# Routing operations of an attention + mixture-of-experts kernel that read one operand from PSUM instead of two from SBUF

## The chip, the cores and the metric

The kernel runs on one core of one Trainium2 chip. The metric is the device time of one execution in microseconds (us); a time is the median of several runs.

## The reference

The first half is chunked attention over 4 batches, 8 heads, 768 positions and head size 64, with chunks of 32 queries, a context of 16 positions to the left and 8 to the right, and 8 memory keys. Its output, as 3072 tokens of 512 values, goes through a mixture of 8 experts. Tokens are assigned greedily: all 3072 x 8 logits are sorted, and each token goes to the first expert on the list that still has room, with 384 tokens per expert:

```python
logits = x @ w_gate
order = np.argsort(-logits.flatten())
for idx in order:
    tok, e = (int(idx) // E, int(idx) % E)
    if assigned[tok] >= 0 or counts[e] >= cap:
        continue
    assigned[tok] = e
    counts[e] += 1
...
for e in range(E):
    mask = assigned == e
    h = np.maximum(x[mask] @ w1[e], 0.0)
    out[mask] = h @ w2[e]
```

## The kernel before

The kernel works in two stages. In the **attention** stage (`attention`, some 105 us) 24 tiles of 128 tokens pass through scores, softmax, the product with the values and the logits; each tile's rows are written to a DRAM tensor `xs`.

In the **expert** stage the 8 experts follow each other. For each expert k, `phase` finds in four rounds of counting (r = 0 to 3) which expert fills up next and at which logit, and then which tokens it gets. All its arithmetic is on VectorE (DVE), with small TensorE (PE) matmuls for sums over partitions. The end of a phase is the part that matters here. It goes, in program order: the masks `oe`, `gq`, `gt`; a running sum over the 24 tiles (the scan, L537); two PE matmuls for the offsets of the partitions (L546, L547); the slot numbers (L552 to L561); and three 0/1 tables: `one` (L564), `lo` (L567) and `hi` (L571). `tokens` multiplies `lo` and `hi` on PE (L586), turns the product into token numbers `ids`, gathers the tokens' rows with GpSimd (POOL) indirect DMAs (L603) and transposes them, for k = 0 on PE (L623), later by DMA (L615).

Meanwhile `weights` converts expert weights: ScalarE (ACT) takes sums of absolute values (L695), PE transposes them (L700), DVE makes a power of two, PE spreads it over the partitions (L707), ACT scales and rounds the weights to fp16 (L728, L730), and POOL subtracts to get the low half (L742; two SBUF inputs of 128x1024 in fp32). `gemm` then runs 96 matmuls into `ps_hid` (L795) and 72 into `ps_y` (L810) per expert; ACT and DVE split the hidden values (L759, L762), DVE scales the output (L770) and POOL scatters it (L818).

The order on every engine is fixed when the program is built. `Lines` holds a generator per activity; each yields an engine, a cost and the time at which it can start, and `Lines.run` takes the line that can start first, ties being broken by the ready time less a lead (`soon`, or the line's own). Costs are estimates of the author; they set the order and nothing else. Each engine executes its queue strictly in this order, so a PE matmul of the routing stands in the same queue as the matmuls of the previous expert's `gemm`. For expert 0, where PE would idle by the plan, `fill` adds matmuls that nobody reads (L426, 128 columns each), written to `g.D[:, 384:512]`.

Two PSUM tiles of one bank each hold the routing's small results. `g.D` is written by PE (counts, sums, offsets, pair products, the weight scales, the fill) and read by DVE and ACT. `g.R` (class `Scratch`) is a work area that only DVE writes and reads. The framework orders accesses to a tile by semaphores.

In five of the operations both tensor inputs lie in SBUF: the scan L537 (`g.one48`, `gq`), `s1` L557 (`slot`, `gt`), `one` L564 (`sm`, `g.io`), `lo` L567 (`one`, `g.idc`) and `hi` L571 (`su`, `g.io`). Most other operations of the routing have one input in `g.R` or `g.D`.

Of the kernel before, what the change touches and what calls it, by code (L numbers as in the profile page):

```python
# [11 lines left out]
F32 = mybir.dt.float32  # L12
F16 = mybir.dt.float16
BF16 = mybir.dt.bfloat16
I32 = mybir.dt.int32
AF = mybir.ActivationFunctionType
ALU = mybir.AluOpType
AX = mybir.AxisListType

P = 128  # L20
# [4 lines left out]
NT = N // P  # L25
DM = H * D
E, FF = 8, 1024
CAP = N // E
# [26 lines left out]
def attention(g):  # L55
# [158 lines left out]
    def hist(i):  # L214
        g.first[1].open(g)
        finish(st["early"])

    def keys(i):
        finish(first_keys(g, i - 3, i + 1))
# [12 lines left out]
    for f, i in ((scores, n), (ptrans, n - 1), (softmax, n), (xtrans, n - 3),  # L232
                 (av, n - 2), (ptrans, n), (logits, n - 4), (rows, n - 3), (av, n - 1), (av, n), (logits2, n - 4),
                 (early, 0), (xtrans, n - 2), (logits, n - 3), (xtrans, n - 1), (logits, n - 2), (early, 1),
                 (xtrans, n), (logits, n - 1), (logits, n), (early, 2), (logits2, n), (hist, 0), (keys, n)):
        f(i)
# [8 lines left out]
class Scratch:  # L245
# [5 lines left out]
                e8=(496, 504), ce=(504, 512),  # L251
                sc=(0, 48), sl=(48, 72), slot=(72, 96), gr=(96, 120))

# [125 lines left out]
class Lines:  # L379
# [42 lines left out]
    def fill(self, t):  # L422
        g = self.g
        n = int((t - self.clk[PE] - 0.25) / 0.17)
        for _ in range(n):
            g.nc.tensor.matmul(g.D[:, 384:512], g.ones, g.fill, start=True, stop=True)  # L426


def phase(g, k, out):
# [6 lines left out]
    def t(shape, dt, tag, bufs=1):  # L436
        return rb.tile(shape, dt, tag=tag, name=tag, bufs=bufs)
# [110 lines left out]

    e = yield DVE, 1.8, max(d, p + LATE)
    sl0 = t([P, NT], F32, "sl0")  # L550
    for a, o in enumerate((sl0, R.sl)):
        v.scalar_tensor_tensor(o, sc[:, a], off[:, a:a + 1], gq[:, a], op0=ALU.add, op1=ALU.mult)  # L552
    slot, row = t([P, NT], F32, "slot"), R.gr
    v.tensor_tensor(slot, R.sl, sl0, op=ALU.add)
    s1 = t([P, NT], F32, "s1")
    v.tensor_scalar(row, slot, -7.5, 0.0625, op0=ALU.add, op1=ALU.mult)
    v.scalar_tensor_tensor(s1, slot, float(CAP), gt, op0=ALU.is_lt, op1=ALU.mult)  # L557
    v.tensor_scalar(row, row, HALF, -HALF, op0=ALU.add, op1=ALU.add)
# [3 lines left out]
    e = yield DVE, 0.85, e  # L562
    one = t([P, 6, 16, 4], BF16, "one")
    v.tensor_tensor(one, sm.rearrange("p (j c) -> p j c", c=4).unsqueeze(2).to_broadcast([P, 6, 16, 4]),  # L564
                    g.io[:, 0:16, 0:4].unsqueeze(1).to_broadcast([P, 6, 16, 4]), op=ALU.is_equal)
    lo = t([P, 6, 2, 16, 4], BF16, "lo")
    v.tensor_tensor(lo, one.unsqueeze(2).to_broadcast([P, 6, 2, 16, 4]),  # L567
                    g.idc.unsqueeze(3).to_broadcast([P, 6, 2, 16, 4]), op=ALU.mult)
    e = yield DVE, 0.4, e
    hi = t([P, NT, NT], BF16, "hi")  # L570
    v.tensor_tensor(hi, su.unsqueeze(1).to_broadcast([P, NT, NT]), g.io[:, 1:NT + 1], op=ALU.is_equal)  # L571
    g.lines.add(tokens(g, k, out, lo, hi, e), 0.4)
# [6 lines left out]
def tokens(g, k, out, lo, hi, e):  # L579
# [3 lines left out]
    p = yield PE, 0.45, e + SEM, soon  # L583
    pair = g.D[:, 132:228]
    for j in range(0, NT, 4):
# [25 lines left out]
    for a in range(NG):  # L611
# [7 lines left out]
        bank = "CBA"[a]  # L619
        p = yield PE, 0.55, lambda: max(g.lines.free(bank), at[a]), soon  # L620
        px = g.lines.take(bank, [P, 2 * KC, P], "ps_xg", F16)
# [64 lines left out]
def weights(g, k, st, n):  # L686
# [5 lines left out]
    for j in range(4):  # L692
        t = yield ACT, 1.25, lambda: fl[j][1] if len(fl) > j else INF, due
        jk = g.wbuf.tile([P, 1024], F16, tag="jk16", name="jk16", bufs=1)
        nc.scalar.activation(jk, fl[j][0], AF.Abs, accum_out=am[:, j:j + 1])  # L695
    soon = 0.0 if k else 5.0
    t = yield DVE, 0.15, t + SEM, soon
    v.tensor_reduce(am[:, 4:5], am[:, 0:4], axis=AX.X, op=ALU.max if n == "1" else ALU.add)
    t = yield PE, 0.12, t + SEM
    nc.tensor.transpose(g.D[0:1, 256:256 + P], am[:, 4:5], g.ident)  # L700
# [4 lines left out]
    pr = pow2(g, rb, m, [1, 1], top, name, bufs=1)  # L705
    t = yield PE, 0.1, t + SEM
    nc.tensor.matmul(g.D[:, 128:130], g.one_row, pr.rearrange("p a b -> p (a b)"), start=True, stop=True)  # L707
    t = yield ACT, 0.17, t + LATE
    s = rb.tile([P, 2], F32, tag=name + "s", name=name + "s", bufs=3)
    nc.scalar.activation(s, g.D[:, 128:130], AF.Copy)  # L710
    st["s" + n] = s
# [138 lines left out]
def constants(g, consts):  # L850
# [15 lines left out]
    def cast(n, dt, rows=P):  # L866
        t = g.fixed.tile([rows, c[n].shape[1]], dt, name="c_" + n)
        nc.gpsimd.tensor_copy(t, c[n][:rows])
        return t
# [6 lines left out]
    nc.gpsimd.memset(g.rz, 0.0)  # L876
    g.idc = cast("idc", BF16).rearrange("p (j x c) -> p j x c", x=2, c=4)
    g.put = cast("put", BF16)
# [7 lines left out]
    nc.vector.memset(R.z0, 0.0)  # L886
    g.one48 = g.fixed.tile([P, 2 * NT], F32, name="one48")
    nc.vector.memset(g.one48, 1.0)
    nc.vector.memset(g.one48[:, NT:NT + 1], 0.0)
    nc.vector.tensor_copy(R.e8, g.e8)  # L890
    g.io = g.fixed.tile([P, NT + 1, NT], BF16, name="io")
    g.fill = g.io[:, 0:6].rearrange("p a b -> p (a b)")[:, 0:128]
    for a, b in ((0, 13), (13, NT + 1)):
        yield
        nc.gpsimd.tensor_copy(g.io[:, a:b], c["io"][:, a:b].unsqueeze(2).to_broadcast([P, b - a, NT]))

# [153 lines left out]
```

## Time and profile before

| | |
|---|---|
| median of 3 runs | 483.92 us (482.54 to 483.98) |
| the profiled execution | 480.79 us, of it 479.0 us span from the first to the last instruction |
| PE busy, whole span | 410.0 us (86%) |
| ACT, DVE, POOL busy | 311.4, 302.6 and 255.8 us |
| attention, span start to about 105 us | DMA bound (share 0.92 in its first 103 us) |
| routing of expert 0 alone | about 105 to 155 us, mean PE clock 0.60 |
| experts | about 155 to 470 us, then the last rows leave |

The times below are us from the start of the span. The clock is the granted TensorE clock, where 1.00 is 2.4 GHz and 0.50 is 1.2 GHz. A row of a timeline gives the start, the duration, the engine, the line, the operation, output <- inputs, shapes, the count of merged instructions and, in brackets, the idle time of the engine before it and what ended it.

### The profile page before, as it was taken

The page shows a single profiled execution, that of the slowest core. Times are in us where ns is not written, and L with a number is a line of the kernel's source. Part 1 is how long each engine was busy: PE and PEld are TensorE (multiplying, and loading weights), DVE is VectorE, ACT ScalarE, POOL GpSimd, SP SyncE. Part 2 cuts the span into 40 slices and gives each one's busy share as a digit, 9 for nine tenths or more (in the row PEclk, how much of TensorE's full clock was granted, in tenths as well). Part 3 has the DMA queues.
Part 4 walks back from the last instruction along what each step waited for, and adds up shares of the span by engine and source line. Part 5 has one row for each costly group of instructions (what it writes and reads, how often), then busy time and mean ns, then how long its engine had stood idle before and what let it go on. Part 6 is the DMA issues. An engine that isn't in the chain of part 4 may idle for free.

```text
span 479.0 us, 10637 instructions
## 1 busy us (share of the span) xinstructions
PE 410.0 (86%) x4024; PEld 245.7 (51%) x4024; DVE 302.6 (63%) x1056; ACT 311.4 (65%) x493; POOL 255.8 (53%) x257
## 2 busy tenths in 40 slices
PE   1979888883677989799998998899799699999992
PEld 1767666672555544355454454445445354645540
DVE  5566666567576579768679778867966962222210
ACT  5487677664007859946947857686689489896500
POOL 6086886772503602971754476266539428956410
PEclk9999999997555899999998999899899899999997
DMA  7999999930136337709709716542850955970001
GB/s 247 356 370 355 351 351 342 377 133 23 68 108 186 125 107 288 154 2 328 200 23 349 158 45 241 189 98 83 313 133 29 349 117 140 361 95 35 22 22 44
DMA packets 41491, 87.60 MB, mean 183 GB/s; under 512 B 25184, under 2 KB 25312, under 8 KB 38496
## 3 DMA queue, kind: packets, MB, share of 16 engines
q1 hardware_dynamic: 35392, 67.58, 43.7%
q0 software_dynamic: 5760, 18.90, 11.9%
q8 instruction: 31, 0.51, 0.4%
q10 hardware_dynamic: 288, 0.44, 0.2%
q14 instruction: 20, 0.16, 0.1%
HBM read 68.81 MB, written 12.60 MB: 170 GB/s over the span
## 4 chain that ended last, share of the span: by engine, by line
PE 54%; DVE 14%; DMA 13%; issue 9%; POOL 6%; ACT 2%; SPq 1%; POOLq 0%; DVEq 0%
PE ps_hid L795 19%; PE ps_y L810 19%; DMA kvb<-in_kv_dram 11%; PE ps_s L103 3%; PE ps_av L137 2%; PE D L369 2%; POOL w2l L742 2%; PE ps_pt L122 2%; DVE R L537 1%; POOL w1l L742 1%; DVE one L564 1%; DMA w1f<-in_w_dram 1%; DVE hl L762 1%; PE D L490 1%; POOL out_dram L818 1%
## 5 line engine op out<-in xcount | busy, mean ns | idle before, releaser
L795 PE MATMUL ps_hid<-x,w1h 128*128 128x384 f16 x512 | 104.8, 340 | 0.0
L742 POOL TENSOR_TENSOR w1l<-w1f,w1h 128x1024 f16<-128x1024 f32 (+1 forms) x33 | 68.0, 2072 | 22.3 <-ACT w1h L730 21.9
L742 POOL TENSOR_TENSOR w2l<-w2f,w2h 128x1024 f16<-128x1024 f32 x28 | 59.2, 2127 | 23.1 <-ACT w2h L730 23.0
L603 POOL DMA_INDIRECT xg<-xs,ids x24 | 23.4, 973 | 84.5 <-DVE R L310 21.1
L759 ACT ACTIVATE hh<-ps_hid 128x384 f16<-128x384 f32 x64 | 31.1, 487 | 55.6 <-PE ps_hid L795 55.2
L795 PEld LDWEIGHTS <-w1h 128*128 128x128 f16 x512 | 49.3, 101 | 32.7 <-issue 5.2
L795 PE MATMUL ps_hid<-x,w1l 128*128 128x384 f16 x256 | 56.8, 341 | 0.0
L810 PEld LDWEIGHTS <-hh 128*128 128x128 f16 x384 | 35.7, 99 | 39.9 <-issue 4.2
L762 DVE SCALAR_TENSOR_TENSOR hl<-ps_hid,hh 128x384 f16<-128x384 f32 x64 | 35.2, 551 | 26.1 <-ACT hh L759 26.0
L810 PE MATMUL ps_y<-w2h,hh 128*128 128x512 f16 x192 | 49.3, 391 | 1.1 <-ACT w2h L730 1.0
L695 ACT ACTIVATE jk<-w1f 128x1024 f16<-128x1024 f32 x32 | 33.7, 1052 | 24.5 <-DMA w1f<-in_w_dram 23.9
L810 PE MATMUL ps_y<-w2l,hh 128*128 128x512 f16 x192 | 49.3, 380 | 0.3 <-DVE w2l L752 0.3
L810 PE MATMUL ps_y<-w2h,hl 128*128 128x512 f16 x192 | 48.1, 381 | 0.0
L818 POOL DMA_INDIRECT out_dram<-y,ids x24 | 23.9, 994 | 39.5 <-DVE y L770 20.2
L103 PE MATMUL ps_s<-kvb 128*32 128x128 f32 x768 | 28.7, 293 | 17.0 <-DMA kvb<-in_kv_dram 16.7
L770 DVE TENSOR_SCALAR y<-ps_y,inv,xg 128x512 f32<-128x512 f32 x24 | 19.3, 805 | 32.8 <-PE ps_y L810 32.6
L171 POOL TENSOR_TENSOR xr<-x,sxp 128x512 f32<-128x512 f32 x24 | 25.1, 1044 | 27.5 <-DVE sxp L654 17.4
L728 ACT ACTIVATE w1f<-w1f,s1s 128x1024 f32<-128x1024 f32 (+1 forms) x33 | 36.7, 1111 | 0.6
L730 ACT ACTIVATE w1h<-w1f 128x1024 f16<-128x1024 f32 (+1 forms) x33 | 34.0, 1029 | 1.2
L695 ACT ACTIVATE jk<-w2f 128x1024 f16<-128x1024 f32 x32 | 33.7, 1052 | 0.9
L173 POOL TENSOR_TENSOR row<-xr,row 128x512 f16<-128x512 f32 x24 | 27.9, 1160 | 11.6 <-issue 4.3
L795 PEld LDWEIGHTS <-w1l 128*128 128x128 f16 x256 | 25.1, 102 | 16.7 <-issue 3.1
(183 smaller groups left out, 778.3 us busy)
## 6 DMA issues: line engine op xcount, KB each, us to landing
kvb<-in_kv_dram SPq DMA_DIRECT2D x46, 580.0 KB, 7.7
w1f<-in_w_dram SPq DMA_DIRECT2D x32, 512.0 KB, 5.9
w2f<-in_w_dram SPq DMA_DIRECT2D x32, 512.0 KB, 8.5
xs<-row POOLq DMA_DIRECT2D x24, 256.5 KB, 7.4
kvb<-in_kv_dram SPq DMA_DIRECT2D x2, 320.0 KB, 3.5
kvb<-in_kv_dram SPq DMA_DIRECT2D x2, 260.0 KB, 4.4
xg<-xs,ids POOLq DMA_INDIRECT x24, 3.6
out_dram<-y,ids POOLq DMA_INDIRECT x24, 2.8
```

Of the source, the lines that this page charges most:

```text
L103: nc.tensor.matmul(o, s["q"][:, pr, c, :], s["k"][:, :, 2 * pr + c // 2, 0:2 + c % 2:1 + c % 2], start=True, stop=True, tile_position=(0, ...
L171: nc.gpsimd.tensor_tensor(xr, s["x"], sx[:, 0].to_broadcast([P, DM]), op=ALU.mult)
L173: nc.gpsimd.tensor_tensor(row[:, DM:2 * DM], xr, row[:, 0:DM], op=ALU.subtract)
L695: nc.scalar.activation(jk, fl[j][0], AF.Abs, accum_out=am[:, j:j + 1])
L728: nc.scalar.activation(fc, fc, AF.Copy, scale=s[:, 0:1])
L730: nc.scalar.activation(hc, fc, AF.Copy, scale=s[:, 0:1] if whole else 1.0)
L742: g.nc.gpsimd.tensor_tensor(l, f, h, op=ALU.subtract)
L759: g.nc.scalar.activation(hh[:, f], ph[:, 0:CAP], AF.Relu)
L762: g.nc.vector.scalar_tensor_tensor(hl[:, f], ph[:, 0:CAP], 0.0, hh[:, f], op0=ALU.max, op1=ALU.subtract)
L795: nc.tensor.matmul(ph[:, 0:CAP], w[:, f // 2, kc, (f % 2) * P:(f % 2) * P + P], st[x][:, kc, :], start=(n == 0), stop=(n == 3 * KC - 1))
L810: nc.tensor.matmul(py, h[:, f, c], w[:, f, :], start=(n == 0), stop=(n == 3 * FC - 1))
L818: sc = g.nc.gpsimd.indirect_dma_start(out=g.out, in_=y, in_offset=None, out_offset=bass.IndirectOffsetOnAxis(ap=ids, axis=0))
```

## The change

Each of the five operations gets one input from PSUM. The slot numbers are computed twice, once into `g.R` (new column range in the formerly unused `slot`) and once into SBUF; `row` and `s1` read the one in `g.R`. The constants for the scan go to `g.D[:, 204:252]`, a table with each value four times (`quads`) to `g.D[:, 448:480]`, written by ACT at the end of attention because logits use those columns before, and `idc` to `g.R`. `hi` uses the table of pairs that `g.R` already holds. The big SBUF table `io` goes; POOL makes two smaller ones. In `g.D` the pair product and the scale's spread move to other columns. The fill matmuls have 64 columns, and the plan counts 0.12 us for each instead of 0.17. Three planned costs change (1.8 to 2.0, 0.55 to 1.05; both are estimates for the order), and for expert 0 the steps of the scales get a lead of 6.0, over the 5.0 of `tokens`.

```diff
+    def quads(i):
+        nc.scalar.activation(g.D[:, 448:480], g.quads0.rearrange("p n t -> p (n t)").bitcast(F32), AF.Copy)
...
-                 (xtrans, n), (logits, n - 1), (logits, n), (early, 2), (logits2, n), (hist, 0), (keys, n)):
+                 (xtrans, n), (logits, n - 1), (logits, n), (early, 2), (logits2, n), (quads, 0), (hist, 0), (keys, n)):
...
-        n = int((t - self.clk[PE] - 0.25) / 0.17)
+        n = int((t - self.clk[PE] - 0.25) / 0.12)
         for _ in range(n):
-            g.nc.tensor.matmul(g.D[:, 384:512], g.ones, g.fill, start=True, stop=True)
+            g.nc.tensor.matmul(g.D[:, 384:448], g.ones, g.fill, start=True, stop=True)
...
-    e = yield DVE, 1.8, max(d, p + LATE)
+    e = yield DVE, 2.0, max(d, p + LATE)
...
+    v.tensor_tensor(R.slot, R.sl, sl0, op=ALU.add)
     v.tensor_tensor(slot, R.sl, sl0, op=ALU.add)
     s1 = t([P, NT], F32, "s1")
-    v.tensor_scalar(row, slot, -7.5, 0.0625, op0=ALU.add, op1=ALU.mult)
-    v.scalar_tensor_tensor(s1, slot, float(CAP), gt, op0=ALU.is_lt, op1=ALU.mult)
+    v.tensor_scalar(row, R.slot, -7.5, 0.0625, op0=ALU.add, op1=ALU.mult)
+    v.scalar_tensor_tensor(s1, R.slot, float(CAP), gt, op0=ALU.is_lt, op1=ALU.mult)
...
+    pairs = g.io2.rearrange("p (n t) -> p n t", t=2)
     v.tensor_tensor(one, sm.rearrange("p (j c) -> p j c", c=4).unsqueeze(2).to_broadcast([P, 6, 16, 4]),
-                    g.io[:, 0:16, 0:4].unsqueeze(1).to_broadcast([P, 6, 16, 4]), op=ALU.is_equal)
+                    g.quads.unsqueeze(1).to_broadcast([P, 6, 16, 4]), op=ALU.is_equal)
...
-                    g.idc.unsqueeze(3).to_broadcast([P, 6, 2, 16, 4]), op=ALU.mult)
+                    R.idc.bitcast(BF16).rearrange("p (j x c) -> p j x c", x=2, c=4).unsqueeze(3).to_broadcast([P, 6, 2, 16, 4]), op=ALU.mult)
...
-    v.tensor_tensor(hi, su.unsqueeze(1).to_broadcast([P, NT, NT]), g.io[:, 1:NT + 1], op=ALU.is_equal)
+    v.tensor_tensor(hi.rearrange("p n (j t) -> p n j t", t=2),
+                    su.rearrange("p (j t) -> p j t", t=2).unsqueeze(1).to_broadcast([P, NT, NT // 2, 2]),
+                    pairs[:, 1:NT + 1].unsqueeze(2).to_broadcast([P, NT, NT // 2, 2]), op=ALU.is_equal)
...
-    pair = g.D[:, 132:228]
+    pair = g.D[:, 108:204]
...
-        p = yield PE, 0.55, lambda: max(g.lines.free(bank), at[a]), soon
+        p = yield PE, 1.05, lambda: max(g.lines.free(bank), at[a]), soon
...
-    soon = 0.0 if k else 5.0
+    soon = 0.0 if k else 6.0
...
-    t = yield PE, 0.12, t + SEM
+    t = yield PE, 0.12, t + SEM, soon
...
-    t = yield PE, 0.1, t + SEM
-    nc.tensor.matmul(g.D[:, 128:130], g.one_row, pr.rearrange("p a b -> p (a b)"), start=True, stop=True)
-    t = yield ACT, 0.17, t + LATE
+    t = yield PE, 0.1, t + SEM, soon
+    nc.tensor.matmul(g.D[:, 106:108], g.one_row, pr.rearrange("p a b -> p (a b)"), start=True, stop=True)
+    t = yield ACT, 0.17, t + LATE, soon
...
-    g.idc = cast("idc", BF16).rearrange("p (j x c) -> p j x c", x=2, c=4)
+    idc = cast("idc", BF16)
...
-    g.one48 = g.fixed.tile([P, 2 * NT], F32, name="one48")
+    nc.vector.tensor_copy(R.idc.bitcast(I32), idc.bitcast(I32))
+    g.one48 = g.D[:, 204:252]
...
-    g.io = g.fixed.tile([P, NT + 1, NT], BF16, name="io")
-    g.fill = g.io[:, 0:6].rearrange("p a b -> p (a b)")[:, 0:128]
-    for a, b in ((0, 13), (13, NT + 1)):
-        yield
-        nc.gpsimd.tensor_copy(g.io[:, a:b], c["io"][:, a:b].unsqueeze(2).to_broadcast([P, b - a, NT]))
+    g.fill = cast("io", BF16)[:, 0:64]
+    g.quads = g.D[:, 448:480].bitcast(BF16).rearrange("p (n t) -> p n t", t=4)
+    quads = g.fixed.tile([P, 16, 4], BF16, name="quads")
+    nc.gpsimd.tensor_copy(quads, c["io"][:, 0:16].unsqueeze(2).to_broadcast([P, 16, 4]))
+    g.quads0 = quads
+    yield
```

## Rows read from the trace of the kernel before

**Rows 1.** The waits of PE between 240 and 406 us (who waited for whom: us in total, times, longest us).

```profile
PE D L586 <- DVE hi L571: 8.5, 3, 3.8
PE D L546 <- DVE rz L538: 4.8, 1, 4.8
```

**Rows 2.** Busy time in five stretches: the 3.4 us behind each of four idle times of PE, and 34 us with the products of expert 6. Columns: length, then busy us and instructions of PE, PEld, DVE, ACT and POOL, then the granted clock, the DMA share and GB/s.

```profile
260.50:263.90 3.40, 3.39 (x15) 1.69 (x15) 2.39 (x9) 1.12 (x2) 0.00 (x0) 0.50 0.87 354
301.50:304.90 3.40, 3.40 (x16) 1.67 (x14) 2.79 (x10) 2.18 (x4) 0.03 (x1) 0.50 0.31 128
342.40:345.80 3.40, 3.40 (x14) 1.70 (x12) 3.23 (x13) 2.12 (x4) 1.07 (x2) 0.51 0.54 219
376.60:380.00 3.40, 2.85 (x11) 1.37 (x11) 3.19 (x16) 0.67 (x2) 0.17 (x1) 0.50 0.99 358
406.00:440.00 34.00, 34.00 (x186) 18.03 (x185) 9.66 (x25) 28.00 (x42) 25.10 (x19) 1.00 0.69 178
```

**Rows 3.** The instructions of the five lines, one per expert: min/median/max in ns, first and last start.

```profile
L537 DVE TENSOR_TENSOR_SCAN R<-one,gq x8: 266/267/5811, 138.4 to 384.1; 128x48 f32<-128x48 f32 x8
L557 DVE SCALAR_TENSOR_TENSOR s<-slot,gt x8: 173/175/1591, 140.4 to 388.1; 128x24 f32<-128x24 f32 x8
L564 DVE TENSOR_TENSOR one<-sm,io x8: 347/354/2200, 141.0 to 389.6; 128x384 bf16<-128x384 bf16 x8
L567 DVE TENSOR_TENSOR lo<-one,c_idc x8: 557/558/2516, 141.4 to 390.0; 128x768 bf16<-128x768 bf16 x8
L571 DVE TENSOR_TENSOR hi<-su,io x8: 436/449/2243, 141.8 to 391.7; 128x576 bf16<-128x576 bf16 x8
```

**Rows 4.** Timeline of the end of the phase of expert 3, DVE and PE.

```profile
254.50 1.59 DVE L557 SCALAR_TENSOR_TENSOR s<-slot,gt 128x24 f32<-128x24 f32 x1
256.88 2.15 DVE L564 TENSOR_TENSOR one<-sm,io 128x384 bf16<-128x384 bf16 x1
260.00 0.45 DVE L571 TENSOR_TENSOR hi<-su,io 128x576 bf16<-128x576 bf16 x1
260.51 0.64 PE L586 MATMUL D<-hi,lo 128*128 128x96 bf16 x6 [2.19 <-DVE hi L571]
```

**Rows 5.** The same of expert 4, DVE, POOL and PE.

```profile
293.34 1.51 DVE L557 SCALAR_TENSOR_TENSOR s<-slot,gt 128x24 f32<-128x24 f32 x1
295.64 2.15 DVE L564 TENSOR_TENSOR one<-sm,io 128x384 bf16<-128x384 bf16 x1
297.83 2.52 DVE L567 TENSOR_TENSOR lo<-one,c_idc 128x768 bf16<-128x768 bf16 x1
300.74 0.44 DVE L571 TENSOR_TENSOR hi<-su,io 128x576 bf16<-128x576 bf16 x1
297.82 2.12 POOL L742 TENSOR_TENSOR w2l<-w2f,w2h 128x1024 f16<-128x1024 f32 x1 [0.23 <-ACT w2h L730]
301.24 0.46 PE L586 MATMUL D<-hi,lo 128*128 128x96 bf16 x6 [3.83 <-DVE hi L571]
```

**Rows 6.** The same of expert 5, DVE and PE.

```profile
336.03 2.20 DVE L564 TENSOR_TENSOR one<-sm,io 128x384 bf16<-128x384 bf16 x1
339.20 2.24 DVE L571 TENSOR_TENSOR hi<-su,io 128x576 bf16<-128x576 bf16 x1
341.50 0.42 PE L586 MATMUL D<-hi,lo 128*128 128x96 bf16 x6 [2.46 <-DVE hi L571]
```

**Rows 7.** The same of expert 6, DVE, POOL and PE.

```profile
371.09 5.81 DVE L537 TENSOR_TENSOR_SCAN R<-one,gq 128x48 f32<-128x48 f32 x1
370.49 6.28 POOL L742 TENSOR_TENSOR w2l<-w2f,w2h 128x1024 f16<-128x1024 f32 x3
377.15 0.16 PE L546 MATMUL D<-rz,c_upper 128*128 128x2 bf16 x1 [4.76 <-DVE rz L538]
```

**Rows 8.** Operations with one input in PSUM. First two rows of the timeline in the phase of expert 5 (POOL and DVE); then all instructions of the first table of the counts, L357, which reads bf16 from `g.R` (min/median/max in ns; the shortest form has 128 elements, the most frequent 768).

```profile
332.79 2.13 POOL L742 TENSOR_TENSOR w2l<-w2f,w2h 128x1024 f16<-128x1024 f32 x1 [0.44 <-ACT w2h L730]
333.17 0.22 DVE L540 TENSOR_TENSOR R<-R,gq 128x48 f32<-128x48 f32 x1
L357 DVE TENSOR_TENSOR ob<-le,R x29: 221/544/555, 112.6 to 365.4; 128x768 bf16<-128x768 bf16 x27, 128x640 bf16<-128x640 bf16 x1, 128x128 bf16<-128x128 bf16 x1
```

**Rows 9.** Timeline of the phase of expert 0, PE and DVE: 12 count matmuls of 64 columns, fill matmuls of 128 columns, and what stands around them.

```profile
125.34 0.97 PE L369 MATMUL D<-ob,oa 128*128 128x64 bf16 x12 [0.24 <-DVE oa L357]
137.11 1.33 PE L426 MATMUL D<-io,ones 128*128 128x128 bf16 x11 [0.26 <-DVE nm L505]
138.94 0.16 PE L546 MATMUL D<-rz,c_upper 128*128 128x2 bf16 x1 [0.50 <-DVE rz L538]
138.42 0.27 DVE L537 TENSOR_TENSOR_SCAN R<-one,gq 128x48 f32<-128x48 f32 x1
140.11 2.29 PE L426 MATMUL D<-io,ones 128*128 128x128 bf16 x20 [0.98 <-DVE R L552]
140.97 0.36 DVE L564 TENSOR_TENSOR one<-sm,io 128x384 bf16<-128x384 bf16 x1
142.35 0.64 PE L586 MATMUL D<-hi,lo 128*128 128x96 bf16 x6
151.43 0.58 PE L707 MATMUL D<-s1p,one_row 1*128 1x2 f32 x2
```

**Rows 10.** The transposes of the weight sums on PE, which write `g.D` (min/median/max in ns, first and last start).

```profile
L700 PE MATMUL D<-ident,am x16: 269/273/373, 148.3 to 434.6; 128*1 128x128 f32 x16
```

More of the change, by code (lines that the diff above doesn't have):

```diff
@@ L251 @@
                 e8=(496, 504), ce=(504, 512),
-                sc=(0, 48), sl=(48, 72), slot=(72, 96), gr=(96, 120))
+                sc=(0, 48), sl=(48, 72), slot=(72, 96), gr=(96, 120),
+                idc=(472, 496))
     def __init__(self, tile):
@@ L705, in weights @@
     pr = pow2(g, rb, m, [1, 1], top, name, bufs=1)
-    t = yield PE, 0.1, t + SEM
-    nc.tensor.matmul(g.D[:, 128:130], g.one_row, pr.rearrange("p a b -> p (a b)"), start=True, stop=True)
-    t = yield ACT, 0.17, t + LATE
+    t = yield PE, 0.1, t + SEM, soon
+    nc.tensor.matmul(g.D[:, 106:108], g.one_row, pr.rearrange("p a b -> p (a b)"), start=True, stop=True)
+    t = yield ACT, 0.17, t + LATE, soon
     s = rb.tile([P, 2], F32, tag=name + "s", name=name + "s", bufs=3)
-    nc.scalar.activation(s, g.D[:, 128:130], AF.Copy)
+    nc.scalar.activation(s, g.D[:, 106:108], AF.Copy)
     st["s" + n] = s
```

## The prediction

> **What bounds the kernel now.** I read four views in this order. First the waits of PE between 240 and 406 us, because PE's queue runs nearly unbroken from the first expert to the end: in these 166 us PE loses its time almost only at two lines, 8.5 us in three waits at L586 and 4.8 us in one at L546, both of them routing matmuls that wait for DVE [rows 1]. The reader is to see that the matmuls of the experts are not waiting for weights: no weight stands in the list. Second, the busy times of stretches: behind each of the four idle times PE runs some 3.4 us at a granted clock of 0.50 or 0.51, which is the 1.2 GHz level, although it is busy; with no such idle time it has 1.00 over 34 us and is busy for all of them, while ACT has 28.00 and POOL 25.10 us of work [rows 2]. So an idle PE pays twice. Third, the rows of the five lines that the change edits: each is short and steady but for a few executions. The scan takes 0.27 us in the median and 5.81 at most, s1 0.18 and 1.59, one 0.35 and 2.20, lo 0.56 and 2.52, hi 0.45 and 2.24 [rows 3]. Fourth, the timelines of the four phases. In that of expert 4, lo starts at 297.83, POOL's subtraction started at 297.82 and ends at 299.94, and lo ends at 300.35: it took about the rest of POOL's time, and then its own [rows 5]. In that of expert 6 the scan starts at 371.09 inside three subtractions that stand back to back from 370.49 to 376.77, and ends at 376.90 [rows 7]. So a stretched operation is one with two SBUF inputs that starts while a POOL subtraction runs, and it waits until POOL is through. Operations with an input in PSUM do not: L540, with as many elements as the scan, takes its 0.22 us in the middle of a subtraction [rows 8], and the 29 tables of L357 never exceed 0.555 us [rows 8].
>
> **The change, part by part.**
>
> *The stretch goes.* All five operations now have at most one SBUF input. For the four phases I ask whether PE's wait goes with it. Expert 3: s1 and one are 1.41 and 1.80 us longer than their medians, 3.2 in all, and PE waits 2.19 for hi [rows 3, 4]. Expert 4: s1, one and lo are longer by 1.33, 1.80 and 1.96, 5.1 in all, against a wait of 3.83 [rows 3, 5]. Expert 5: one and hi are longer by 1.85 and 1.79, 3.6 in all, against 2.46 [rows 3, 6]. Expert 6: the scan is longer by 5.54, against 4.76 [rows 3, 7]. In each the excess is larger than the wait, by 0.8 to 1.3 us, so hi and rz will be ready before PE comes to the matmul. Gain: 2.19 + 3.83 + 2.46 + 4.76 = 13.24 us. What is late next is nothing within 0.8 us; after that, PE's own queue.
>
> *The clock behind it.* Half speed over 3.4 us costs 1.7 us for a PE that is busy throughout, as in the first three stretches, and 1.4 in the fourth, where it is busy for 2.85 [rows 2]: 6.5 us. From below: nothing, if a shorter wait remains in the same places and the clock falls all the same. I take 6.5, since the wait that precedes each fall goes.
>
> *Reading bf16 tables from PSUM.* Nearest row: ob of L357 reads a bf16 table in PSUM and takes 0.221 us for 128 elements and 0.544 for 768, 0.50 ns per element [rows 8]. lo with 768 elements and both inputs in SBUF takes 0.557 [rows 3]. So I cost the move at nothing; all three new patterns have two or four neighbouring elements innermost, as L357 has. The Trainium skill (VectorE: DVE Perf Modes, "The perf-mode tier table") speaks against the change here: it lists tensor_tensor with any PSUM operand at one element per cycle, half of what it gives for bf16 in SBUF. By that the sum would be about 1 us higher at expert 0 and, at worst, 7 us higher over all experts; the rows of L357 do not agree with it.
>
> *The second slot operation.* One more DVE operation of 24 elements per expert, at most the 0.18 us of s1 [rows 3], 1.4 us in 8 phases. In the experts above DVE has 0.8 us and more in hand, which hides it; uncovered it would cost all 1.4. At expert 0 it lies on the path: 0.2.
>
> *New order in D.* The fill writes other columns of D than DVE reads, yet in the rows it starts only when DVE has finished reading: behind nm before L546, behind L552 before L586 [rows 9]. So accesses are ordered per tile, not per column. The change makes two more operations read D, the scan and one, and both stand ahead of a fill in program order. The fill's matmuls become shorter but more: 11 at 0.17 planned are 15 or 16 at 0.12, and 20 are, with the 0.2 us added to the plan, about 30. At half clock 12 matmuls of 64 columns take 0.97 us [rows 9], about 0.075 each behind the first: 1.2 and 2.25 us. The first fill, 137.11 to 138.44 so far, starts when the scan ends at 138.69, ends near 139.9, and L546 starts 1.0 late; then one, so far ending at 141.33, ends near 142.4, the second fill near 144.7, and L586 starts 2.3 us after its 142.35 [rows 9]. Behind it stand token numbers, gathers, transposes, and the first product of expert 0. Other phases have no fill. From below: nothing, if the fill is dropped or falls elsewhere; from above 2.3.
>
> *The first scale's lead.* The spread L707 now runs at 151.43, between the transposes of gathered rows [rows 9]; with the lead it stands ahead of them and ACT can begin the first weights earlier. Since the gather is now the later of the two, this gives back little: I take 0.7 of the 2.3, which leaves 1.6 for expert 0, between -0.7 and 2.3.
>
> *Setup.* One ACT copy at the end of attention, one DVE copy and smaller POOL casts during it. The copies have 32 and 24 elements per partition, like s1 (0.18) [rows 3]; DVE's keys for the last tiles cover the first, DMA the others. Uncovered: 0.4. Queues of SP and of POOL's gathers keep their order; no DMA is added.
>
> *The sum.* 480.79 for the profiled execution, less 13.24 and 6.5, plus 1.6 and 0.2, is 462.85. The median of the runs shown lies 3.13 above the profiled one, and I keep that distance: 466.0.
>
> **The rivals.**
>
> *PE waits for something else.* PE now asks for weights some 5 us earlier per expert, and ACT or POOL becomes the bound. Against it: the 34 us in which PE is full while ACT and POOL keep up [rows 2]; an expert with its routing will take about 36. For it: changed costs change the fixed order of everything behind expert 0, and any new wait also costs clock. If half of the 19.74 is lost, the time is 475.9.
>
> *Half-rate tables.* The table operations run at one element per cycle. One more 0.50 ns for each of 1728 elements is 0.9 us per expert; PE's 0.8 to 1.3 us in hand hide part of it. All eight on the path would be 7.2, hence 473.2.
>
> *Slower: D orders PE behind DVE.* The weight scales' matmuls, 16 transposes and 16 spreads, write D too [rows 10]. One that the new order puts between L546 and L586 must now wait for one, with the experts' matmuls queued behind it. From L546 to the end of one are 2.4 us at expert 0 [rows 9]; with a fall of the clock, 4.1 us. It decides from five such matmuls on: 5 x 4.1 = 20.5 eats the gain, and seven give about 495. Against it: where the plan puts two such steps so near is chance, since they belong to different experts.
>
> *The change does not do what it says.* If the stretch comes from writing or from POOL's wait for semaphores, it stays, and only the new costs do: 483.92 + 1.8 = 485.7. Against it: the operations of rows 8 write SBUF and PSUM, and neither is stretched.
>
> **How the numbers follow.** Forecast 0.72; PE waits for something else 0.15; half rate 0.05; order in D 0.04; stretch stays 0.04. Differences under 0.3%, 1.5 us, are about what a measurement here cannot tell from none. The first three cases are faster: 0.92. Order in D is slower, 0.04; the staying stretch I split evenly, 0.02 slower and 0.02 the same. So 0.92, 0.02, 0.06. The range: below, expert 0 at -0.7 (2.3 less), no extra slot cost, the full 6.8 us of clock, and runs that lie as near as the profiled one (3.1 less) would make 460; above, the rival with half of the gain lost, 475.9. I give 460 to 475.
>
> **What would show it.** Right: no row of the five lines above 0.6 us; no PE idle time above 0.8 us at L586 or L546 of experts 3 to 6; granted clock 1.00 behind them; POOL's subtractions still 2.13 us; L546 and L586 of expert 0 later by 1.0 and 2.3 us, with their fills behind the scan and one. Wrong: a stretched row with an input in PSUM; one, lo or hi near 0.55, 0.94 and 0.74 us, which is half rate; new waits of PE on weights or at L700 and L707; a later first product of expert 0 by more than 2.3 us.

## The result and the profile after

The changed kernel takes 465.73 us in the median (462.53 to 466.44, 4 runs), the kernel before 483.95 (482.54 to 485.74, 4 runs): ratio 0.9609, interval 0.9552 to 0.9665. The prediction was 466.0. Ratios and intervals here and below leave out executions more than 1.5% above the fastest of their kernel (one of operands_back, 478.1 us, and a few of the kernel before). The profiled execution took 462.53 us with a span of 460.8, against 480.79 and 479.0 before. In both traces the last matmul of attention ends at the same place (L137, at 107.37 and 107.30), so the two compare directly.

First the waits of PE from 240 to 390 us, after the change (us in total, times, longest). They answer to [rows 1].

```profile
PE D L494 <- DVE hs L482: 0.3, 1, 0.3
PE D L708 <- DVE am L706: 0.2, 1, 0.2
```

The 13.3 us of [rows 1] are gone and nothing has taken their place. The stretches from expert 2's products to expert 6's, in the columns of [rows 2]:

```profile
242.00:280.00 38.00, 37.73 (x273) 20.42 (x274) 29.60 (x115) 29.09 (x42) 24.53 (x19) 1.00 0.54 174
280.00:317.00 37.00, 36.65 (x256) 19.73 (x255) 28.60 (x114) 29.44 (x42) 22.99 (x17) 1.00 0.58 178
317.00:354.00 37.00, 36.94 (x259) 19.98 (x256) 27.89 (x111) 32.63 (x47) 22.63 (x16) 1.00 0.57 179
354.00:388.00 34.00, 33.98 (x212) 18.20 (x211) 21.01 (x86) 28.57 (x42) 21.61 (x18) 1.00 0.71 210
388.00:422.00 34.00, 34.00 (x186) 18.06 (x185) 9.67 (x25) 28.85 (x44) 25.09 (x19) 1.00 0.58 179
```

PE is busy throughout and the clock is 1.00 in every row; ACT's 32.63 in 37 us is the nearest that another engine comes. The five edited lines (min/median/max in ns), to be held against [rows 3]:

```profile
L541 DVE TENSOR_TENSOR_SCAN R<-D,gq x8: 265/265/266, 137.8 to 368.9; 128x48 f32<-128x48 f32 x8
L562 DVE SCALAR_TENSOR_TENSOR s<-R,gt x8: 181/182/182, 140.5 to 373.3; 128x24 f32<-128x24 f32 x8
L570 DVE TENSOR_TENSOR one<-sm,D x8: 330/342/354, 141.1 to 375.2; 128x384 bf16<-128x384 bf16 x8
L573 DVE TENSOR_TENSOR lo<-one,R x8: 553/554/555, 141.5 to 375.5; 128x768 bf16<-128x768 bf16 x8
L577 DVE TENSOR_TENSOR hi<-su,R x8: 443/444/447, 142.0 to 376.0; 128x576 bf16<-128x576 bf16 x8
```

Maximum and median now agree, to 0.012 us. That is not because these operations no longer run beside a POOL subtraction (a meeting, in what follows). In the timeline of expert 3, which answers to [rows 4], `one` and `lo` run inside one, and `hi` starts 0.07 us before its end (256.54 + 2.13 = 258.67):

```profile
256.54 2.13 POOL L750 TENSOR_TENSOR w2l<-w2f,w2h 128x1024 f16<-128x1024 f32 x1 [0.90 <-ACT w2h L738]
257.28 0.34 DVE L570 TENSOR_TENSOR one<-sm,D 128x384 bf16<-128x384 bf16 x1
257.66 0.55 DVE L573 TENSOR_TENSOR lo<-one,R 128x768 bf16<-128x768 bf16 x1
258.60 0.44 DVE L577 TENSOR_TENSOR hi<-su,R 128x576 bf16<-128x576 bf16 x1
260.03 0.42 PE L594 MATMUL D<-hi,lo 128*128 128x96 bf16 x6
```

The last row has no bracket: `hi` ended at 259.04, PE came at 260.03. In experts 4 to 6 the same distance is 0.72, 0.91 and 0.97 us. At L550 of expert 6, where the wait had been, `rz` (L542) is ready 0.67 us before PE comes. At expert 0 (answers to [rows 9]) the order in `g.D` costs something:

```profile
125.08 0.97 PE L373 MATMUL D<-ob,oa 128*128 128x64 bf16 x12 [0.50 <-DVE oa L361]
129.35 0.96 PE L373 MATMUL D<-ob,oa 128*128 128x64 bf16 x12 [0.50 <-DVE oa L361]
...
137.82 0.27 DVE L541 TENSOR_TENSOR_SCAN R<-D,gq 128x48 f32<-128x48 f32 x1
138.14 1.01 PE L430 MATMUL D<-c_io,ones 128*128 128x64 bf16 x16 [1.89 <-DVE R L541]
138.97 0.19 PE L550 MATMUL D<-rz,c_upper 128*128 128x2 bf16 x1
139.79 0.19 DVE L558 TENSOR_TENSOR R<-R,sl 128x24 f32<-128x24 f32 x1
...
141.12 0.35 DVE L570 TENSOR_TENSOR one<-sm,D 128x384 bf16<-128x384 bf16 x1
141.53 1.76 PE L430 MATMUL D<-c_io,ones 128*128 128x64 bf16 x30 [2.35 <-DVE one L570]
143.10 0.67 PE L594 MATMUL D<-hi,lo 128*128 128x96 bf16 x6
...
150.87 0.58 PE L715 MATMUL D<-s1p,one_row 1*128 1x2 f32 x2
```

The fills now start behind the scan and behind `one`, as their brackets say. Where the span went, for all traces of this case: the end of attention, from there to the first `ps_hid` matmul of expert 0, from that to expert 1's, from that to expert 7's, and from that to the end of the span.

```
us                 attention  to expert 0's  to expert  experts  expert 7
                   ends       products       1's        1 to 6   to the end
before             107.30     47.56          47.19      236.77   40.18
after              107.37     48.81          47.45      216.95   40.17
operands_only      113.09     48.18          48.01      216.26   40.17
operands_back      109.67     47.80          48.44      223.07   40.17
scan_back          110.83     48.55          46.50      218.15   40.17
tables_back        109.24     48.30          48.90      220.34   40.17
pool_writes        109.59     47.70          47.24      217.76   40.17
idle_added         111.40     48.81          48.38      238.28   40.18
no_lead            112.12     48.90          47.18      217.23   40.17
no_fill            109.83     44.66          46.68      216.78   40.17
fill_rounds_only   108.75     49.79          47.04      216.53   40.17
before_cost        112.68     49.32          48.29      223.08   40.17
before_order       108.66     49.92          46.68      236.96   40.17
before_no_fill     111.54     43.99          47.69      236.23   40.17
```

From before to after, experts 1 to 6 become 19.82 us shorter, expert 0 takes 1.25 longer and the stretch behind it 0.26. The end of attention moves by up to 5.8 us from trace to trace, and by 5.4 between before and before_cost, whose attention is the same; the other columns are free of that, so they are compared below beside the medians.

### The profile page after: what moved, and what is told of

Its sections match the earlier page's. It is cut to its first block, busy times and chain, and to the rows that moved or that the text cites. A ratio compares the mean times of both kernels' runs of the same rounds, so it can differ in the third digit from the quotient of the medians.

```text
span 460.8 us, 10742 instructions
## 1 busy us (share of the span) xinstructions
PE 398.0 (86%) x4072; PEld 241.9 (53%) x4072; DVE 287.6 (62%) x1065; ACT 311.0 (68%) x494; POOL 255.6 (55%) x257
## 4 chain that ended last, share of the span: by engine, by line
PE 63%; DMA 15%; issue 8%; DVE 5%; POOL 4%; ACT 2%; SPq 1%; POOLq 0%; DVEq 0%
PE ps_hid L803 25%; PE ps_y L818 23%; DMA kvb<-in_kv_dram 13%; PE D L373 3%; PE ps_s L103 3%; PE ps_av L137 2%; POOL w2l L750 2%; PE ps_pt L122 2%; DMA w1f<-in_w_dram 1%; PE D L494 1%; PE D L715 1%; POOL out_dram L826 1%; PE ps_xt L181 1%; DMA xg<-xs,ids 1%; ACT w2h L738 1%
## 5 line engine op out<-in xcount | busy, mean ns | idle before, releaser
L803 PE MATMUL ps_hid<-x,w1h 128*128 128x384 f16 x512 | 100.2, 331 | 0.0
L803 PEld LDWEIGHTS <-w1h 128*128 128x128 f16 x512 | 48.2, 99 | 30.1 <-issue 1.2
L803 PE MATMUL ps_hid<-x,w1l 128*128 128x384 f16 x256 | 54.8, 332 | 0.0
L103 PEld LDWEIGHTS ps_s<-kvb 128*32 128x32 f32 x768 | 22.8, 116 | 22.6 <-issue 15.8
```

The lines of the kernel that those rows point to most:

```text
L103: nc.tensor.matmul(o, s["q"][:, pr, c, :], s["k"][:, :, 2 * pr + c // 2, 0:2 + c % 2:1 + c % 2], start=True, stop=True, tile_position=(0, ...
L803: nc.tensor.matmul(ph[:, 0:CAP], w[:, f // 2, kc, (f % 2) * P:(f % 2) * P + P], st[x][:, kc, :], start=(n == 0), stop=(n == 3 * KC - 1))
```

## Experiments

**The theory**: a DVE operation with two SBUF inputs waits for POOL operations that read SBUF; PE, which waits for it, idles and then runs at half clock. **The rivals**: the new costs alone change the order and with it the meetings; the matter is POOL being busy, whatever it does; the idle time is not what the 20 us are made of. The kernel before was run again beside each set of experiments (medians 485.09 to 486.37 us), and the ratios below are to those runs.

**All five operands back in SBUF** (operands_back; the order, the lead and the fill of after kept):

```diff
-    v.tensor_tensor(one, ..., g.quads...)      # and scan, s1, lo, hi alike
+    v.tensor_tensor(one, ..., g.io[:, 0:16, 0:4]...)
```

> The changed kernel in which the five operations read two SBUF inputs again; the order, the fill, the lead and the second slot operation stay. Theory (a DVE operation with two SBUF inputs waits for a running POOL subtraction, PE idles and its clock falls): rows of scan, s1, one, lo and hi up to 1.5 to 6 us in experts 3 to 6, PE idle of 2 us and more at L594 or L550 there, clock near 0.5 behind it, 480 to 486 us. Rival (the changed costs and the lead made a better order): near 466 us. At expert 0 the fills start about 1 us earlier than in the changed kernel, since scan and one no longer read D.

Measured: 471.02 us (466.64 to 478.1), ratio to before 0.9667 (0.9573 to 0.9761). The theory as stated missed: three scans, two s1 and three `one` are stretched again (a scan of 2.58 us, a `one` of 2.15), yet PE waits only 3.2 us for `hi` and 1.5 for `rz` (240 to 406 us, the two largest):

```profile
PE D L592 <- DVE hi L577: 3.2, 3, 2.0
PE D L550 <- DVE rz L542: 1.5, 1, 1.5
```

The granted clock behind each of these waits is 1.00. That the planned costs had moved PE's queue is followed below. At expert 0, where scan and `one` no longer read `g.D` and the fills are the same, L550 comes 0.60 us and L594 1.09 earlier behind the end of attention than in after (about 1 was expected).

**The operands alone** (operands_only: after, with the costs 1.8, 0.55 and 0.17 of before and no lead):

```diff
-        n = int((t - self.clk[PE] - 0.25) / 0.12)
+        n = int((t - self.clk[PE] - 0.25) / 0.17)
-    e = yield DVE, 2.0, max(d, p + LATE)
+    e = yield DVE, 1.8, max(d, p + LATE)
...
-        p = yield PE, 1.05, ...
+        p = yield PE, 0.55, ...
```

> The five operations read PSUM as in the changed kernel, but planned costs, the lead and the number of fill matmuls are those of before (each fill has 64 columns, since the other columns now hold a table). Theory: 464 to 468 us, no stretched row. Rival (order): 480 to 484 us.

Measured: 466.56 us (463.45 to 467.56), 0.9598 (0.9528 to 0.9668). No stretched row, no wait of PE for a routing operation above 0.34 us between 240 and 400, experts 1 to 6 in 216.26. The operands give the whole gain without the new order.

**The scan alone back, and the tables alone back**:

```diff
-    g.one48 = g.D[:, 204:252]                            # scan_back
+    g.one48 = g.fixed.tile([P, 2 * NT], F32, name="one48")
```

> Only the scan reads SBUF twice again. Theory: in the changed kernel's timeline the scans of experts 4, 5 and 6 start 0.43, 0.65 and 0.37 us before a subtraction ends, so they take 0.6 to 0.9 us in place of 0.27; PE comes to L550 0.8 us after the scan or later, so PE waits little and the time stays within 1 us of 466. Rival (any stretched operation costs its length): 1.5 us more than 466.

Measured: 465.5 us (464.25 to 466.47), 0.9592 (0.9529 to 0.9655). Of the five lines only the scan is stretched, to 0.56, 0.77 and 2.58 us, the last because a second subtraction followed the one that it met: the miss is that 0.9 was expected. PE waits 1.54 us for it at L550, at a clock of 1.00 behind it, and experts 1 to 6 are 1.2 longer.

```diff
-                    g.quads...   R.idc...   pairs[:, 1:NT + 1]...     # one, lo, hi: tables_back
+                    g.io[:, 0:16, 0:4]...   g.idc...   g.io[:, 1:NT + 1]...
```

> Only one, lo and hi read SBUF twice again. Theory: by the changed kernel's timeline one of expert 3 would wait 1.4 us, one of expert 4 1.9 and its lo perhaps another, hi of expert 5 2.0; PE has about 0.9 us in hand, so it idles 0.5 to 3 us in two or three phases, each with 1.7 us of clock where the clock falls: 472 to 478 us. Rival (order): 466.

Measured: 467.67 us (466.9 to 468.72), 0.9637 (0.9576 to 0.9697): smaller than expected. `one` takes 1.60, 2.15 and 0.71 us, `hi` 1.92; PE's five idle times are 0.18 to 0.99 us, 2.6 in all, with no fall of the clock; experts 1 to 6 are 3.4 longer.

**POOL writes instead of reading** (pool_writes: the kernel before; for experts 1 to 7 a subtraction of `w2` becomes one of a single element and three memsets, so the low half of w2 is left out):

```diff
-    g.nc.gpsimd.tensor_tensor(l, f, h, op=ALU.subtract)
+    if n == "2" and part == 1.0:
+        g.nc.gpsimd.tensor_tensor(l[0:1, 0:1], f[0:1, 0:1], h[0:1, 0:1], op=ALU.subtract)
+        for _ in range(3):
+            g.nc.gpsimd.memset(l, 0.0)
+    else:
+        g.nc.gpsimd.tensor_tensor(l, f, h, op=ALU.subtract)
```

> The kernel before, but from expert 1 on POOL does not compute the low half of w2: in place of each subtraction it subtracts one element and then writes the low half three times with a memset (so the low half of w2 is left out of the result). Theory (the operation waits because both need the same way of reading SBUF): memsets only write, so the five operations keep their medians even where they run beside one, PE does not idle at L586 and L546 of experts 3 to 6, 464 to 467 us. Rival (any running POOL instruction holds a two-input DVE operation, or a semaphore does): stretched rows up to the length of the memsets, 475 to 485 us.

Measured: 464.9 us (463.87 to 467.75), 0.9599 (0.9534 to 0.9664). The operands are those of before, and the timeline of expert 3 (POOL and DVE) has them inside POOL's work:

```profile
256.94 2.97 POOL L745 MEMSET w2l<- 128x1024 f16 x3
257.75 0.35 DVE L564 TENSOR_TENSOR one<-sm,io 128x384 bf16<-128x384 bf16 x1
258.13 0.56 DVE L567 TENSOR_TENSOR lo<-one,c_idc 128x768 bf16<-128x768 bf16 x1
259.08 0.45 DVE L571 TENSOR_TENSOR hi<-su,io 128x576 bf16<-128x576 bf16 x1
```

Two SBUF inputs, POOL busy for 2.97 us, and each row takes its own time. So it is not POOL's being busy that holds them. POOL's gathers do not hold them either: in before, `s1`, `one` and `lo` of expert 7 take 0.17, 0.35 and 0.56 us beside L603. That it is the subtraction's reading of SBUF fits all of this, but no experiment sets another operation of POOL that reads as much in its place. The Trainium skill (SBUF — State Buffer, "Who interferes with whom") puts it down to the reading: such an instruction contends with a GpSimd instruction that reads SBUF, not with one that only writes it. The trace agrees for the memsets.

**Idle time put back** (idle_added: after, with one DVE reduction ahead of `hi` in experts 3 to 6):

```diff
+    if 3 <= k <= 6:
+        gap = t([P, 22], F32, "gap")
+        v.tensor_reduce(gap, La...to_broadcast([P, 22, NT * E]), axis=AX.X, op=ALU.max)
```

> The changed kernel with one DVE reduction of 4224 elements, about 4.4 us, before hi in experts 3 to 6; it has one SBUF input and does not meet POOL. PE has some 1 us in hand, so it idles about 3.4 us at L594 in each of the four. Theory (an idle PE pays twice): four stretches of 3.4 us at clock 0.50 behind it, 13.6 + 6.8 = 20 us more than 466, that is 486. Rival (idle is paid once, and the fall of the clock has another cause): 13.6 more, 479 to 480.

Measured: 486.88 us (484.08 to 488.81, 10 runs), 1.0034 (0.9998 to 1.007) to before. PE's wait, then the 3.4 us behind each of the four (columns of [rows 2]):

```profile
PE D L597 <- DVE hi L580: 13.9, 4, 3.6
```

```profile
268.46:271.86 3.40, 3.40 (x16) 1.74 (x16) 3.11 (x12) 1.45 (x3) 0.12 (x1) 0.57 0.53 213
309.51:312.91 3.40, 3.40 (x18) 1.96 (x18) 3.08 (x12) 0.08 (x1) 0.34 (x1) 0.59 0.49 198
350.01:353.41 3.40, 3.40 (x17) 1.90 (x17) 2.90 (x12) 1.45 (x3) 0.00 (x0) 0.52 0.51 205
391.89:395.29 3.40, 3.40 (x16) 1.84 (x16) 2.48 (x12) 1.45 (x3) 0.00 (x0) 0.50 0.47 189
...
395.29:398.69 3.40, 3.40 (x16) 1.61 (x15) 0.81 (x5) 2.16 (x5) 0.06 (x1) 0.65 0.01 2
```

The fifth row stands directly behind the fourth. The clock that is missing in these five rows, 3.4 us times 0.43, 0.41, 0.48, 0.50 and 0.35, is 7.4 us; with 13.9 of idle time 21.3. Experts 1 to 6 are 238.28 - 216.95 = 21.3 us longer. Idle time of PE here is paid about 1.5 times in the sum of the four, and that closes the account. A single one can be paid once, as before_no_fill shows below.

**Without the lead, without the fill**:

```diff
-    soon = 0.0 if k else 6.0                              # no_lead, and its three yields
+    soon = 0.0 if k else 5.0
```

> The changed kernel without the lead of the first scales. Theory (the gather is the later of the two at expert 0): first product later by 0 to 0.7 us, 466 to 467 us. Rival (the lead is worth its 1.5 us of earlier scale): 467.5 us or more.

Measured: 467.08 us (461.75 to 468.63), 0.9614 (0.9555 to 0.9673). From the end of attention to the last matmul 344.62 us against 344.52: the lead is worth nothing. L715, which it was to bring forward, starts 43.5 us behind attention in both.

```diff
-        n = int((t - self.clk[PE] - 0.25) / 0.12)        # no_fill
+        n = 0
```

> The changed kernel without any fill matmul. Theory (the fill of expert 0 now stands behind the scan and one and holds back L594): L594 of expert 0 starts near 142.5 in place of 143.1, rounds of counting 0.3 us shorter each, first product of expert 0 earlier by about 1.5 to 2.5 us, 463 to 465 us. Rival (the fill keeps the clock up or brings it back sooner): no gain or a loss of 1 to 2 us.

Measured: 459.81 us (457.56 to 463.49, 6 runs), 0.948 (0.9425 to 0.9535): the best of all kernels here, faster than before and after. Two of its counts (L373), then the stretch of expert 0's routing, without the fill and with it:

```profile
126.27 0.96 PE L373 MATMUL D<-ob,oa 128*128 128x64 bf16 x12 [1.61 <-DVE oa L361]
...
130.07 0.97 PE L373 MATMUL D<-ob,oa 128*128 128x64 bf16 x12 [1.61 <-DVE oa L361]
```

```profile
112.00:158.00 46.00, 17.93 (x175) 12.81 (x174) 33.92 (x153) 16.12 (x31) 14.81 (x18) 0.55 0.36 122
```

```profile
112.00:158.00 46.00, 23.94 (x290) 19.53 (x291) 31.85 (x145) 15.06 (x29) 13.98 (x17) 0.58 0.34 110
```

A round takes 3.80 us instead of 129.35 - 125.08 = 4.27, 0.39 of it because no fill stands in front of L494 and L505 (0.05 us from DVE's end to each, instead of 0.24 and 0.25); and the fill had brought the clock from 0.55 to 0.58 only (from the end of attention to expert 0's first product, from 0.57 to 0.62). Expert 0's products begin 4.15 us earlier.

**Which part of the fill** (fill_rounds_only: no fill ahead of L550 and L594):

```diff
-            if eng == PE and t < self.g.cold and not self.g.open:
+            if eng == PE and t < self.g.cold and not self.g.open and cost not in (0.06, 0.45):
```

> The changed kernel without the two groups of fill that stand behind the scan and behind one at expert 0 (and without the same group before expert 0's other pair products); the fill of the counting rounds stays. Theory (those two groups cost the 0.9 us that L594 gained over the counting in the run without fill): 464 to 465.5 us. Rival (all of the 5 us comes from them): 460 to 461.

Measured: 463.88 us (462.21 to 466.28), 0.9611 (0.9562 to 0.9659). L594 comes 34.84 us behind attention instead of 35.73, but expert 0's products do not come earlier (49.79 against 48.81): between them PE waits 2.1 us for weight sums at L708 and 1.9 for gathered rows, in after 1.2 and 1.4. The 1.9 hold a wait of 1.39 for the third gather, which after does not have, so this one execution does not settle what the two groups cost the products. In no_fill the phase's expert is known 26.63 us behind attention, in after 29.28: 2.65 of the 4.15 us lie in the rounds.

**The kernel before with one edit each**. The cost of 1.8 (before_cost):

```diff
-    e = yield DVE, 1.8, max(d, p + LATE)
+    e = yield DVE, 2.0, max(d, p + LATE)
```

> The kernel before with one planned cost changed, 1.8 to 2.0 for the slot operations; the five operations still read SBUF twice. Theory A (this cost moves L586 behind more ps_hid matmuls in PE's queue and shifts the meetings with POOL, which is why the changed order alone was worth 12 us with the operands back): 470 to 476 us. Theory B (the lead and the cost of the transposes made the better order): 482 to 485.

Measured: 472.62 us (470.74 to 475.31), 0.9775 (0.9734 to 0.9816). Its two largest waits of PE, 240 to 400 us, and expert 6's scan (the view starts inside the first of three subtractions that stand back to back):

```profile
PE D L586 <- DVE hi L571: 3.2, 3, 2.0
PE D L546 <- DVE rz L538: 1.5, 1, 1.5
```

```profile
370.84 4.21 POOL L742 TENSOR_TENSOR w2l<-w2f,w2h 128x1024 f16<-128x1024 f32 x2
372.60 2.58 DVE L537 TENSOR_TENSOR_SCAN R<-one,gq 128x48 f32<-128x48 f32 x1
375.43 0.16 PE L546 MATMUL D<-rz,c_upper 128*128 128x2 bf16 x1 [1.54 <-DVE rz L538]
```

This number, which describes no instruction, is worth 11 us in the table above and 12.5 in the medians. Between L547 and L586 of experts 3 to 6 stand 35, 34, 32 and 35 `ps_hid` matmuls instead of 30, 30, 33 and 33. In experts 3 and 4, where PE comes later to `hi`, its waits fall from 2.19 to 0.17 and from 3.83 to 0.98 us; in expert 6 the later scan meets the rest of two subtractions where [rows 7] had three. `one` still takes 2.15 us at worst. Each of the four waits is now 2.04 us or less, and in the 3.4 us behind each of them the granted clock is 1.00.

The lead and the cost of 1.05 instead (before_order; the diff shows the cost):

```diff
-        p = yield PE, 0.55, ...
+        p = yield PE, 1.05, ...
```

> The kernel before with the lead of the first scales and the transposes planned at 1.05 in place of 0.55; the cost 1.8, the fill and the operands stay. Theory A: 482 to 485 us. Theory B: 470 to 476.

Measured: 484.95 us (481.72 to 487.51, 10 runs), 1.0025 (0.9991 to 1.0059): no difference. And no fill (before_no_fill):

```diff
-        n = int((t - self.clk[PE] - 0.25) / 0.17)
+        n = 0
```

> The kernel before without any fill matmul. Theory (the fill stands in the way of the counting matmuls of expert 0 in both kernels, some 0.66 us per round): first product of expert 0 earlier by 2.5 to 3.5 us after the end of attention, four idle times of PE in experts 3 to 6 as before, 480 to 482 us where before has 484 to 485. Rival (the fill is costly only because scan and one now read D): gain under 1.5 us.

Measured: 481.54 us (478.2 to 484.59, 10 runs), 0.9939 (0.9894 to 0.9984): the fill cost the kernel before some 3 us too (0.8 to 5.1 by the interval). PE's waits are those of [rows 1], but at expert 5 the clock does not fall behind one; the end of the wait, and the 3.4 us behind it:

```profile
342.76 0.33 PE L586 MATMUL D<-hi,lo 128*128 128x96 bf16 x4 [2.46 <-DVE hi L571]
```

```profile
342.76:346.16 3.40, 3.40 (x27) 2.17 (x27) 3.26 (x13) 1.73 (x4) 0.47 (x1) 1.00 0.74 300
```

It stays at 1.00 up to 374.8, where the same 2.46 us in [rows 2, 6] are followed by a fall to 0.51. So the length of the wait alone does not say whether the clock falls. Expert 5's stretch is 1.69 us shorter for it; expert 6's is 1.05 longer, because there the clock stays low for 5.0 us behind the wait instead of 2.85, and so the sum of experts 1 to 6 hardly differs (236.23 against 236.77).

## Why the prediction was right, and where it was not

*The stretch and the clock: right, in place and nearly in size.* Predicted for experts 3 to 6: 19.74 us less. Measured: 20.47 less from expert 2's first product to expert 7's, and 0.65 more from expert 1's to expert 2's, which leaves the 19.82. The 0.65 come with the cost of 2.0: the stretch takes 38.06 us in before and 37.97 in operands_only, 38.64 in before_cost and 38.71 in after. The time in hand, forecast as 0.8 to 1.3 us, is 0.7 to 1.0 in after; in operands_only, whose order is the one that was reckoned with, it is 0.60, 0.60 and 0.65 at L594 of experts 3 to 5 and 0.67 at L550 of expert 6. It sufficed, and PE's own queue is next, as was said. The operands alone bring the gain (operands_only), they had waited for POOL's subtractions and not for its memsets (pool_writes), and the idle time with its clock has that price (idle_added).

*Tables from PSUM: right.* `one`, `lo` and `hi` take 0.342, 0.554 and 0.444 us against 0.354, 0.558 and 0.449 in [rows 3]. By the rule that the Trainium skill (VectorE: DVE Perf Modes, "The perf-mode tier table") gives for a tensor_tensor with a PSUM operand, the prediction's estimate for them was 0.55, 0.94 and 0.74; the measurement decides against it.

*The second slot operation: too small.* From the first of them to `one` are 1.33 us at expert 0 (139.79 to 141.12), before 0.88 (to `one` at 140.97 from this row):

```profile
140.09 0.18 DVE L554 TENSOR_TENSOR slot<-R,sl 128x24 f32<-128x24 f32 x1
```

That is 0.45 instead of 0.2: now that `row` and `s1` also touch `g.R`, each starts 0.22 us after the one before it, where `s1` had started after 0.10.

*The order in D: the mechanism right, the size not.* The fills moved behind the scan and `one`, with 16 and 30 matmuls as forecast, but L550 is 0.03 us later and L594 0.75, not 1.0 and 2.3. Two terms were off: a fill matmul takes 1.76 / 30 = 0.059 us, not 0.075, and the rounds of counting, left out of the sum, became shorter with the shorter fill, so that the phase's expert is known 0.6 us earlier (the end of L516 at 136.65, of L512 at 137.24 before). Against the same rounds and fills without the order in D, operands_back, the cost is 0.60 us at L550 and 1.09 at L594.

*The lead: nothing, not 0.7.* Together with the fills, 1.6 was forecast for expert 0 and the slot operation 0.2; its first product is 1.25 later than before, and 0.26 follow: 1.5 against 1.8, with each of the three terms off.

*What the prediction did not see.* Its last rival, in which the stretch stays and the costs alone act, was given 485.7 us. That state is nearly operands_back, and takes 471.0. The prediction named the changed order only as a risk; it had no term for more matmuls ahead of L586, which shorten PE's wait whatever DVE does. So either edit alone takes most of the time away: the cost 13.7 us (before_cost, experts 1 to 6), the operands 20.5, both 19.8. The sum came out because the operands remove all of the wait in either order. That it came out within 0.3 us is luck: the terms of expert 0 are off and partly cancel, and the forecast rests on the median lying 3.13 us above the profiled run, which it did again (3.20), while in the twelve other kernels it lies between 2.7 below and 0.5 above.

*Still open*: which instruction of the plan the 0.2 us of cost moves first was not followed, and why expert 0's first product varies by 2 us between kernels with like routing (47.56 in before, 49.92 in before_order) is known in part. L586 stands 35.05 and 35.06 us behind attention in these two; they part at the gathered rows, where PE waits 1.37 us for the third gather in before_order and not at all in before. Why that transfer came later is open.

## What to carry to other kernels

When an operation's maximum is far above its median, look at what another engine did in those moments, and hold each excess against the wait of the engine that sets the pace; where all excesses exceed the waits, the waits go whole. A planned cost in a fixed order is a part of the change like any instruction: run it alone, since it can give most of the gain by shifting a queue and so hide or mimic the cause. Work that is put in to keep an engine warm stands in that engine's queue; take it out once and time it.

## What the runs showed of the hardware

- A DVE operation with two SBUF inputs waits out POOL subtractions that stand back to back: the scan took 5.81 us behind the rest of three [rows 7], 2.58 behind the rest of two (scan_back, before_cost). With one input in PSUM it took 0.265 to 0.266 (after). POOL's memsets, 0.95 us each, delayed none (pool_writes). The subtractions themselves kept 2.13 us in the median and took 2.19 at most (operands_back).
- PE's clock was 0.50 or 0.51 behind idle times of 2.19, 2.46, 3.83 and 4.76 us in before [rows 2, 4, 5, 6, 7], and 1.00 behind 2.04, 1.54 and 0.98 (before_cost); but behind 2.46 us in before_no_fill it was 1.00.
- Matmuls that filled the waits of expert 0's rounds raised the clock from 0.57 to 0.62 there (from the end of attention to expert 0's first product, no_fill and after) and cost 5.1 us (from the end of attention to the end of the span, 353.4 us with them, 348.3 without).
